# Scaling v on another engine, turning one pair later, and column tiles for the products of a lightning-attention kernel

## Chip, cores and metric

One core of one Trainium2 chip. The metric is device microseconds (us) of one execution; "span" is the time from the first to the last instruction in the trace, some 2 us less than the run's time. Runs of this program on one core scatter by up to 3%: the kernel before took 107.02 to 110.07 us in its first runs. Each comparison therefore uses runs of both kernels on the same chip, and runs more than 1.5% above the fastest of their kernel are left out as slow.

## The reference

Attention with decay, for 4 batches of 8 heads of 768 rows of 64, then a mixing layer over the tokens of each batch. Cut to what matters:

```python
# attention, per head, in blocks; lam is the head's decay
intra = ((qb @ kb.T) * Dmask) @ vb             # Dmask[i, j] = lam ** (i - j) for i >= j, else 0
inter = (qb * lam_pow) @ kv_state
out[block] = intra + inter
kv_state = lam_block * kv_state + (kb * rev_pow).T @ vb
# mixing, per batch: x is (768 tokens, 512 channels)
W_tok = (x @ w_q) @ (x @ w_k).T / 8
y = relu(W_tok @ x) @ w_out                    # f32, 4 x 768 x 512
```

Both kernels turn the decays into factors on q and v, so that a block needs only a mask of zeros and ones, and both reorder the mixing as `(x w_q) ((x w_k).T x)`.

## The kernel before

Two heads make a pair; there are 16 pairs `n`, four (`kk`) to each batch `b`. For each pair the kernel transposes q and k on TensorE (`turn`: trq, trk), scales v by powers of the decay (`scale_v`: vn), adds up the states (`states`: dps, then gs), multiplies q by k (`scores`: sc, masked to pr on VectorE), and adds `inter` and `values` into oa. `flip` transposes the result (xp to xnat). The mixing of a batch (`mix_...`) is laid among the pairs of the next ones: pq, pk, py, pm, and po, whose tile of 128 tokens is copied to osb and written out. Engines work in program order.

```python
    def scale_v(n, eng):
        ...
        eng.tensor_tensor(out=vn, in0=fv, in1=DvI[...].to_broadcast([128, 2, NCH, D]), op=ALU.mult)

    def mix_po(b, t, last=False):
        po = pst([128, HD], F32, "po")
        for kt in range(4):
            nc.tensor.matmul(po, M[b]["rmT"][:, kt, t * CH : (t + 1) * CH], wo[:, kt, :],
                             start=(kt == 0), stop=(kt == 3))
        osb = outp.tile([128, HD], F32, tag="osb", name="osb")
        ... # copied from po on ScalarE, or VectorE
        nc.sync.dma_start(out=out[b, t * CH : (t + 1) * CH, :], in_=osb)

    for n in range(N):
        b, kk = pairs[n]
        if n + 2 < N:
            take_k(n + 2)
            scale_v(n + 2, nc.gpsimd)          # two pairs ahead, on GpSimd
        if n + AHEAD < N:
            load(n + AHEAD)                    # AHEAD = 5, loads issued by GpSimd
        ...
        scores(n)
        ...
        if n >= 1:
            flip(n - 1)
        ...                                    # pq, py or po of earlier batches
        inter(n)
        values(n)
        if n + 1 < N:
            states(n + 1)
        if n + 2 < N:
            turn(n + 2)                        # two pairs ahead
        ...                                    # pk or pm
    ...                                        # tail: the last batch's mixing, six tiles of po
```

Of the kernel before, what the change touches and what calls it, by code (L numbers as in the profile page):

```python
# [21 lines left out]
AHEAD = 5  # L22
WARM = 11
# [3 lines left out]
def kernel(  # L27
# [14 lines left out]
    stage = ctx.enter_context(tc.tile_pool(name="stage", bufs=9))  # L42
# [7 lines left out]
    ps = ctx.enter_context(tc.tile_pool(name="ps", bufs=8, space=bass.MemoryType.PSUM))  # L50
# [19 lines left out]
    def load_q(n):  # L70
        t = stage.tile([128, 2, 3, 2 * D], BF16, tag="fq", name="fq")
        nc.gpsimd.dma_start(out=t, in_=q_rows(n))  # L72
        staged[n, "q"] = t

    def load_kv(n):
        for nm, src in (("k", k), ("v", v)):
            t = stage.tile([128, 2, NCH, D], BF16, tag="f" + nm, name="f" + nm)
            nc.gpsimd.dma_start(out=t, in_=kv_rows(n, src))  # L78
            staged[n, nm] = t

    def load(n):
        load_q(n)
        load_kv(n)


    load_q(0)
    t0 = stage.tile([128, 2, NCH, D], BF16, tag="fv", name="fv")
    nc.gpsimd.dma_start(out=t0, in_=kv_rows(0, v))
    staged[0, "v"] = t0
    lam_all = consts.tile([128, H], F32, name="lam_all")  # L90
    nc.sync.dma_start(out=lam_all, in_=lam.partition_broadcast(128))
    k0 = consts.tile([128, 2, NCH, D], F32, name="k0")
    nc.sync.dma_start(out=k0, in_=kv_rows(0, k))
    wqk_f = consts.tile([128, 2, 4, DHY], F32, name="wqk_f")
    for i, w in enumerate((moe_w_q, moe_w_k)):
        nc.sync.dma_start(out=wqk_f[:, i], in_=w.rearrange("(kt p) j -> p kt j", p=128))


    nc.scalar.preload_act_table_set("natural_log_exp_and_others")
    blank = consts.tile([128, HD], BF16, name="blank")  # L100
# [40 lines left out]
    load(2)  # L141
    lnl = consts.tile([128, H], F32, name="lnl")
    nc.scalar.activation(out=lnl, in_=lam_all, func=ACT.Ln)
    lnv = lnl.rearrange("p (k l) -> p k l", l=2)
    lncol = consts.tile([128, NP], F32, name="lncol")
    for hl in range(2):
        nc.vector.tensor_copy(
            out=lncol[hl * 64 : hl * 64 + 64, :], in_=lnv[hl * 64 : hl * 64 + 64, :, hl]
        )
# [6 lines left out]
    )  # L156
    Dq = [consts.tile([128, S], BF16, name=f"dq{kk}") for kk in range(NP)]
# [6 lines left out]
    swap = consts.tile([128, 128], BF16, name="swap")  # L164


    wqk = consts.tile([128, 4, 3 * DHY], BF16, name="wqk")
    wo = consts.tile([128, 4, HD], BF16, name="wo")

    def cast_wqk():  # L170
        nc.scalar.copy(out=wqk[:, :, 0:DHY], in_=wqk_f[:, 0])
        nc.scalar.copy(out=wqk[:, :, DHY : 2 * DHY], in_=wqk_f[:, 1])
        nc.scalar.copy(out=wqk[:, :, 2 * DHY :], in_=wqk_f[:, 0])
        nc.vector.tensor_copy(out=swap[:, 0:64], in_=ident[:, 64:128])
        nc.vector.tensor_copy(out=swap[:, 64:128], in_=ident[:, 0:64])

    def load_wo():
        nc.gpsimd.dma_start(out=wo, in_=moe_w_out.rearrange("(kt p) j -> p kt j", p=128))


    L = {}
    xT, xnat = {}, {}

    def take_k(n):
        if n == 0:
            kn = nat.tile([128, 2, NCH, D], BF16, tag="kn", name="kn")
            nc.vector.tensor_copy(out=kn, in_=k0)
        else:
            kn = staged.pop((n, "k"))
        L[n] = dict(kn=kn)  # L190

    def scale_v(n, eng):
        b, kk = pairs[n]
        vn = nat.tile([128, 2, NCH, D], BF16, tag="vn", name="vn")
        fv = staged.pop((n, "v"))
        eng.tensor_tensor(  # L196
            out=vn,
            in0=fv,
            in1=DvI[:, 2 * kk : 2 * kk + 2, :].unsqueeze(3).to_broadcast([128, 2, NCH, D]),
            op=ALU.mult,  # L200
        )
        L[n]["vn"] = vn

    def turn(n):
        b, kk = pairs[n]
        fq, kn = staged.pop((n, "q")), L[n]["kn"]
# [82 lines left out]
    def inter(n):  # L289
        gs = L[n]["gs"]  # L290
        oa = [pst([128, 3, CH], F32, "oa") for a in range(2)]
# [14 lines left out]
    def values(n):  # L306
# [5 lines left out]
        for a in range(2):  # L312
            for cc in range(3):
                c = 3 * a + cc
                for hl in range(2):
# [9 lines left out]
            nc.scalar.copy(  # L325
                out=xT[b][:, kk, a * HALF : (a + 1) * HALF].rearrange(
                    "d (c p r) -> d c r p", c=3, r=2
                ),
                in_=oa[a].rearrange("d c (r p) -> d c r p", r=2),
            )  # L330
        del L[n]

    def flip(n):
        b, kk = pairs[n]
        xp = pst([128, NCH, CH], BF16, "xp")
        for t in range(NCH):
            nc.tensor.transpose(xp[:, t, :], xT[b][:, kk, t * CH : (t + 1) * CH], ident)  # L337
        to = xnat[b][:, :, kk * CH : (kk + 1) * CH]
        if b == 0:
            nc.scalar.copy(out=to, in_=xp)  # L340
        else:
            nc.vector.tensor_copy(out=to, in_=xp)  # L342
# [6 lines left out]
    def mix_pq(b):  # L349
        qkT = hyp.tile([128, S], BF16, tag="qkT", name="qkT")  # L350
        M[b] = dict(qkT=qkT)
        for n in range(2):
            pq = pst([128, HALF], F32, "pq")
            for kt in range(NP):
                nc.tensor.matmul(  # L355
                    pq,
                    wqk[:, kt, n * DHY : n * DHY + 128],
                    xT[b][:, kt, n * HALF : (n + 1) * HALF],
                    start=(kt == 0),
                    stop=(kt == NP - 1),  # L360
                )
            nc.scalar.copy(out=qkT[:, n * HALF : (n + 1) * HALF], in_=pq)

    def mix_pk(b):
        qkT = M[b]["qkT"]
        pk = pst([128, NCH, CH], BF16, "pk")
        for t in range(NCH):
            nc.tensor.transpose(  # L368
                pk[:, t, :], qkT[:, t * CH : (t + 1) * CH], swap if t < 3 else ident
            )  # L370
        wkn = hyp.tile([128, NCH, 2, DHY], BF16, tag="wkn", name="wkn")
        nc.vector.tensor_copy(
            out=wkn, in_=pk[:, :, 0:DHY].unsqueeze(2).to_broadcast([128, NCH, 2, DHY])
        )
        M[b]["wkn"] = wkn

    def mix_py(b, last=False):
        py = pst([128, HD], F32, "py")
        for t in range(NCH):
            nc.tensor.matmul(  # L380
                py,
                M[b]["wkn"][:, t, :, :].rearrange("p i j -> p (i j)"),
                xnat[b][:, t, :],
                start=(t == 0),
                stop=(t == NCH - 1),
            )
        Y = hyp.tile([128, HD], BF16, tag="Y", name="Y")
        if last:
            nc.vector.tensor_copy(out=Y[:, 0:256], in_=py[:, 0:256])  # L389
            nc.scalar.copy(out=Y[:, 256:], in_=py[:, 256:])  # L390
        else:
            nc.scalar.copy(out=Y, in_=py)
# [3 lines left out]
    def mix_pm(b, dds, last=False):  # L396
        pms = {}
        for dd in dds:
            for n in range(2):
                r = slice(n * 64, n * 64 + 64)  # L400
                pm = pst([128, HALF], F32, "pm")
                nc.tensor.matmul(  # L402
                    pm,
                    M[b]["Y"][r, dd * CH : (dd + 1) * CH],
                    M[b]["qkT"][r, n * HALF : (n + 1) * HALF],
                    start=True,
                    stop=True,
                )
                pms[dd, n] = pm
        for n in range(2):  # L410
            for dd in dds:
                to = M[b]["rmT"][:, dd, n * HALF : (n + 1) * HALF]
                if last and dd % 2:
                    nc.vector.tensor_scalar(  # L414
                        out=to,
                        in0=pms[dd, n],
                        scalar1=1.0 / 8.0,
                        scalar2=0.0,
                        op0=ALU.mult,
                        op1=ALU.max,  # L420
                    )
                else:
                    nc.scalar.activation(  # L423
                        out=to, in_=pms[dd, n], func=ACT.Relu, scale=1.0 / 8.0
                    )

    def mix_po(b, t, last=False):
        po = pst([128, HD], F32, "po")
        for kt in range(4):
            nc.tensor.matmul(  # L430
                po,
                M[b]["rmT"][:, kt, t * CH : (t + 1) * CH],
                wo[:, kt, :],
                start=(kt == 0),
                stop=(kt == 3),
            )
        osb = outp.tile([128, HD], F32, tag="osb", name="osb")
        if last and t % 2:
# [3 lines left out]
        nc.sync.dma_start(out=out[b, t * CH : (t + 1) * CH, :], in_=osb)  # L442


    warm = pst([128, HD], F32, "warm")
    for _ in range(WARM):
        nc.tensor.matmul(warm, blank[:, 0:128], blank, start=True, stop=True)
    make_dq(0)
    take_k(0)
    turn(0)  # L450
    scale_v(0, nc.vector)
    states(0)
    make_dq(1)
    take_k(1)
    turn(1)
    load(3)
    scale_v(1, nc.vector)
    make_dq(2)
    load(4)

    for n in range(N):
# [6 lines left out]
        if n == 0:  # L468
            load_wo()
# [72 lines left out]
```

## Time and profile before

108.53 us (median of 3 runs); the profiled run took 107.25 us, with a span of 105.3 us.

| busy, us (share of span) | before |
|---|---|
| TensorE | 90.8 (86%) |
| VectorE | 66.4 (63%) |
| ScalarE | 67.9 (64%) |
| GpSimd | 68.6 (65%) |

The shares are averages over stages with different limits, so the prediction below reads the kernel by stages: a stage is cut where TensorE starts the scores of a batch's first pair.

The transfers themselves, in the view of that tile (line, engine, operation, count: shortest/median/longest issue in ns, first and last start):

```profile
L442 SPq DMA_DIRECT2D out_dram<-osb x24: 332/332/933, 45.6 to 102.1; - x24
```

SyncE issues 24 transfers of 128 rows, in 0.33 us each (one took 0.93), and the last six tiles come 0.91 us apart (5.49 us for the six in the chain). It has time to spare.

### The profile page before, as it was taken

What the parts mean: (1) busy time and instruction counts of PE and PEld (TensorE: products, weight loads), DVE (VectorE), ACT (ScalarE), POOL (GpSimd) and SP (SyncE); (2) the same over time, 40 slices, a digit from 0 to 9 for tenths busy, and PEclk for the clock granted to TensorE, in tenths of its full rate; (3) what the DMA queues carried; (4) which work ended last, traced back from release to release, by engine and by line L of the source; (5) the groups of instructions that cost most, each with busy time, mean ns of one, the idle gap of its engine ahead of it and who ended that gap; (6) DMA issues with size and microseconds to landing.
All of it is one profiled execution on the core that took longest, in us unless ns stands there. A gap on an engine that the chain in (4) does not pass through costs nothing. (4 is left out here: it accounts for less than half of the span.)

```text
span 105.3 us, 3311 instructions
## 1 busy us (share of the span) xinstructions
PE 90.8 (86%) x1403; PEld 58.5 (56%) x1403; DVE 66.4 (63%) x163; ACT 67.9 (64%) x123; POOL 68.6 (65%) x70
## 2 busy tenths in 40 slices
PE   5914878889699999999999999999999999989950
PEld 2213657658567577558757575577575555623410
DVE  2434587997594988918897829198986370237440
ACT  4045097987587397867839788778397868638320
POOL 5999999999999999999999999450410000000000
PEclk9995579999999999999999999999999999999999
DMA  0999999999999999999999999997000706332482
GB/s 15 195 167 165 165 160 166 165 163 166 200 167 167 162 165 162 163 178 219 231 169 162 160 175 233 237 200 242 4 0 6 290 9 253 146 121 84 166 321 111
DMA packets 67406, 16.93 MB, mean 161 GB/s; under 512 B 63808, under 2 KB 64320, under 8 KB 67392
## 3 DMA queue, kind: packets, MB, share of 16 engines
q0 software_dynamic: 61184, 9.77, 124.8%
q1 hardware_dynamic: 6208, 6.95, 19.9%
q8 instruction: 11, 0.18, 0.6%
q14 instruction: 3, 0.02, 0.1%
HBM read 20.19 MB, written 6.29 MB: 251 GB/s over the span
## 5 line engine op out<-in xcount | busy, mean ns | idle before, releaser
L285 DVE TENSOR_TENSOR pr<-sc,maskc 128x384 bf16<-128x384 f32 x64 | 31.1, 549 | 0.8 <-PE sc L273 0.3
L196 POOL TENSOR_TENSOR vn<-fv,DvI 128x768 bf16<-128x768 bf16 x14 | 21.0, 1500 | 7.0 <-DMA fv<-in_v_dram 4.6
L430 PE MATMUL po<-wo,rmT 128*128 128x512 bf16 x96 | 22.3, 379 | 0.0
L325 ACT CAST xT<-oa 128x384 bf16<-128x384 f32 x32 | 17.1, 594 | 2.9 <-PE oa L317 1.7
L230 ACT COPY kT<-trk 128x768 bf16<-128x768 bf16 x16 | 12.8, 798 | 8.5 <-PE trk L226 7.9
L441 ACT COPY osb<-po 128x512 f32<-128x512 f32 x21 | 12.3, 585 | 8.8 <-PE po L430 7.2
L78 POOL DMA_DIRECT2D fk<-in_k_dram x15 | 15.8, 1055 | 0.0
L78 POOL DMA_DIRECT2D fv<-in_v_dram x15 | 15.6, 1041 | 0.0
L72 POOL DMA_DIRECT2D fq<-in_q_dram x16 | 14.2, 889 | 0.8 <-POOLq L526 0.8
L253 DVE COPY two<-dps 128x64 f32<-128x64 f32 x16 | 3.6, 225 | 17.5 <-PE dps L243 17.4
L430 PEld LDWEIGHTS <-rmT 128*128 128x128 bf16 x96 | 9.1, 98 | 9.9 <-DVE rmT L414 0.5
L317 PE MATMUL oa<-pr,vn 128*64 128x128 bf16 x192 | 11.0, 223 | 2.4 <-DVE pr L285 1.7
L423 ACT ACTIVATE rmT<-pm 128x384 bf16<-128x384 f32 x28 | 11.6, 508 | 0.0
L273 PE MATMUL sc<-qT,kT 64*128 64x128 bf16 x192 | 10.3, 223 | 0.9 <-ACT kT L230 0.3
L211 PE MATMUL trq<-ident,fq 128*64 128x128 bf16 x192 | 9.0, 231 | 2.4 <-DMA fq<-in_q_dram 2.4
L217 DVE TENSOR_TENSOR qT<-trq,dq 128x768 bf16<-128x768 bf16 x16 | 8.8, 549 | 2.3 <-PE trq L211 2.2
L317 PEld LDWEIGHTS <-vn 128*64 128x64 bf16 x192 | 6.8, 109 | 5.6 <-issue 4.1
L342 DVE COPY xnat<-xp 128x768 bf16<-128x768 bf16 x12 | 6.6, 549 | 4.9 <-PE xp L337 4.9
L273 PEld LDWEIGHTS <-kT 64*128 64x128 bf16 x192 | 6.8, 96 | 4.0 <-issue 1.9
L337 PE MATMUL xp<-ident,xT 128*128 128x128 bf16 x96 | 8.1, 220 | 0.3
L211 PEld LDWEIGHTS <-fq 128*64 128x64 bf16 x192 | 6.6, 118 | 2.9 <-DMA fq<-in_q_dram 2.9
L226 PE MATMUL trk<-ident,fk 128*64 128x128 bf16 x180 | 8.0, 226 | 0.1
(57 smaller groups left out, 113.5 us busy)
## 6 DMA issues: line engine op xcount, KB each, us to landing
out_dram<-osb SPq DMA_DIRECT2D x24, 256.0 KB, 2.1
fq<-in_q_dram POOLq DMA_DIRECT2D x16, 192.0 KB, 6.8
fv<-in_v_dram POOLq DMA_DIRECT2D x16, 192.0 KB, 8.0
fk<-in_k_dram POOLq DMA_DIRECT2D x15, 192.0 KB, 7.8
wo<-in_moe_w_out_dram POOLq DMA_DIRECT2D x1, 512.0 KB, 9.2
k<-in_k_dram SPq DMA_DIRECT2D x1, 384.0 KB, 4.0
wqk_f<-in_moe_w_q_dram SPq DMA_DIRECT2D x1, 128.0 KB, 6.0
wqk_f<-in_moe_w_k_dram SPq DMA_DIRECT2D x1, 128.0 KB, 7.1
```

What stands on the lines that cost most here:

```text
L72: nc.gpsimd.dma_start(out=t, in_=q_rows(n))
L78: nc.gpsimd.dma_start(out=t, in_=kv_rows(n, src))
L196: eng.tensor_tensor(out=vn, in0=fv, in1=DvI[:, 2 * kk : 2 * kk + 2, :].unsqueeze(3).to_broadcast([128, 2, NCH, D]), op=ALU.mult,)
L211: nc.tensor.transpose(trq[hl * 64 : hl * 64 + 64, a, r, :], fq[:, hl, a, r * D : (r + 1) * D], ident,)
L230: nc.scalar.copy(out=kT, in_=trk)
L273: nc.tensor.matmul(sc[a, hl][:, cc, :], kT[r, c * CH : (c + 1) * CH], qchunk(n, r, c), start=True, stop=True, skip_group_check=True,)
L285: nc.vector.tensor_tensor(out=t, in0=sc[a, hl], in1=maskc, op=ALU.mult)
L317: nc.tensor.matmul(oa[a][r, cc, :], vn[:, hl, c, :], pr[a, hl][:, cc, :], start=False, stop=(cc == 2), skip_group_check=True,)
L325: nc.scalar.copy(out=xT[b][:, kk, a * HALF : (a + 1) * HALF].rearrange("d (c p r) -> d c r p", c=3, r=2), in_=oa[a].rearrange("d c (r p) - ...
L423: nc.scalar.activation(out=to, in_=pms[dd, n], func=ACT.Relu, scale=1.0 / 8.0)
L430: nc.tensor.matmul(po, M[b]["rmT"][:, kt, t * CH : (t + 1) * CH], wo[:, kt, :], start=(kt == 0), stop=(kt == 3),)
L441: nc.scalar.copy(out=osb, in_=po)
```

## The change

Its intent: VectorE takes the scaling of v, and GpSimd only issues loads; q and k are turned one pair ahead instead of two; the flip, the mixing's q and y products and its output products run as pairs of column tiles of TensorE, 64 output rows each; the mixing's k product comes out row-major, so that its transposes go; and what is left of the mixing is spread anew over the pairs.

```diff
-    ps = ctx.enter_context(tc.tile_pool(name="ps", bufs=8, space=bass.MemoryType.PSUM))
+    ps = ctx.enter_context(tc.tile_pool(name="ps", bufs=6, space=bass.MemoryType.PSUM))
+    psx = ctx.enter_context(tc.tile_pool(name="psx", bufs=2, space=bass.MemoryType.PSUM))   # oa
 # --- prologue: k0 through GpSimd, q0 and v0 in f32 through SyncE; cut ---
 # --- scale_v: eng.tensor_tensor -> nc.vector.tensor_tensor; values, two evictions: ---
-            nc.scalar.copy(
-                out=xT[b][:, kk, a * HALF : (a + 1) * HALF].rearrange(
-                    "d (c p r) -> d c r p", c=3, r=2
-                ),
-                in_=oa[a].rearrange("d c (r p) -> d c r p", r=2),
-            )
+            nc.scalar.copy(out=xT[b][:, kk, a * HALF : (a + 1) * HALF], in_=oa[a])
 # --- flip ---
-            nc.tensor.transpose(xp[:, t, :], xT[b][:, kk, t * CH : (t + 1) * CH], ident)
-        to = xnat[b][:, :, kk * CH : (kk + 1) * CH]
-        if b == 0:
-            nc.scalar.copy(out=to, in_=xp)
-        else:
-            nc.vector.tensor_copy(out=to, in_=xp)
+            for i in range(2):
+                o = t * CH + i * 64
+                nc.tensor.transpose(
+                    xp[i * 64 : i * 64 + 64, t, :], xT[b][:, kk, o : o + 64], ident
+                )
+        nc.scalar.copy(out=xnat[b][:, :, kk * CH : (kk + 1) * CH], in_=xp)
 # --- mix_pq, mix_pk -> mix_wk (row-major), mix_wq; mix_py, mix_pm on halves; cut ---
 # --- mix_po: four full products -> eight on column tiles; then the output: ---
-        nc.sync.dma_start(out=out[b, t * CH : (t + 1) * CH, :], in_=osb)
+        rows = out[b, t * CH : (t + 1) * CH, :].rearrange("(p r) d -> r p d", r=2)
+        for r in range(2):
+            nc.sync.dma_start(out=rows[r], in_=osb[r * 64 : r * 64 + 64, :])
 # --- the loop, with the placing of the mixing cut ---
-        if n + 2 < N:
-            take_k(n + 2)
-            scale_v(n + 2, nc.gpsimd)
-        if n + AHEAD < N:
-            load(n + AHEAD)
+        if n + 8 < N:
+            load(n + 8)
         scores(n)
-        if n >= 1:
-            flip(n - 1)
         inter(n)
+        if n + 1 < N:
+            take(n + 1)
+            turn(n + 1)
+            scale_v(n + 1)
+        if n >= 1:
+            flip(n - 1)
         values(n)
         if n + 1 < N:
             states(n + 1)
-        if n + 2 < N:
-            turn(n + 2)
```

The columns of the scores are in the order even rows, then odd rows. The kernel before put them back in order when it evicted oa. The changed one does not, and puts the rows in order with two output transfers for each tile of 128 tokens.

## The prediction

> **What bounds the kernel now.** I first read the page's slices, to see where the span has different limits.
>
> ```profile
> PE   5914878889699999999999999999999999989950
> DVE  2434587997594988918897829198986370237440
> ACT  4045097987587397867839788778397868638320
> POOL 5999999999999999999999999450410000000000
> PEclk9995579999999999999999999999999999999999
> ```
>
> Each digit is 2.6 us. TensorE is full from slice 11 (29 us) to slice 36; before that it has gaps while VectorE is fullest; GpSimd is full to 66 us. Then the timeline of TensorE, which I cut at the first scores of each batch of four pairs: 13.05, 29.18, 48.40 and 69.22 us, end of the last value products at 88.4. The stages are thus 13.05 (prologue), 16.1, 19.2, 20.8, 19.2 and 16.9 us (tail). A pair of the first batch looks like this (start, length, group):
>
> ```profile
> 21.20 0.51 PE L273 MATMUL sc<-qT,kT 64*128 64x128 bf16 x12
> 21.64 0.51 PE L337 MATMUL xp<-ident,xT 128*128 128x128 bf16 x6
> 22.08 0.47 PE L296 MATMUL oa<-qT,gs 64*64 64x128 bf16 x10
> 22.48 0.97 PE L317 MATMUL oa<-pr,vn 128*64 128x128 bf16 x7
> 23.70 0.33 PE L317 MATMUL oa<-pr,vn 128*64 128x128 bf16 x5 [0.25 <-DVE pr L285]
> 23.84 0.44 PE L243 MATMUL dps<-vn,fk 128*64 128x128 bf16 x10
> 24.09 0.53 PE L211 MATMUL trq<-ident,fq 128*64 128x128 bf16 x12
> 24.43 0.52 PE L226 MATMUL trk<-ident,fk 128*64 128x128 bf16 x12
> 24.89 0.51 PE L273 MATMUL sc<-qT,kT 64*128 64x128 bf16 x12
> ```
>
> Scores to scores is 3.69 us. TensorE waits for the four maskings (pr), then must run states and turning before the next scores: a loop through VectorE. Later the wait is gone; an extract of the third batch:
>
> ```profile
> 57.29 0.81 PE L273 MATMUL sc<-qT,kT 64*128 64x128 bf16 x12
> 58.17 0.49 PE L337 MATMUL xp<-ident,xT 128*128 128x128 bf16 x6
> 58.55 2.75 PE L430 MATMUL po<-wo,rmT 128*128 128x512 bf16 x12
> 61.23 0.47 PE L296 MATMUL oa<-qT,gs 64*64 64x128 bf16 x10
> ```
>
> Twelve output products take 2.68 us start to start. Here the sum of TensorE's work is the time. The groups by shape give the durations that I need below:
>
> ```profile
> L285 DVE TENSOR_TENSOR pr<-sc,maskc 128x384 bf16<-128x384 f32 x64 | 31.1, 549 | 0.8 <-PE sc L273 0.3
> L196 DVE TENSOR_TENSOR vn<-fv,DvI 128x768 bf16<-128x768 bf16 x2 | 1.9, 958 | 1.4 <-DMA fv<-in_v_dram 1.4
> L196 POOL TENSOR_TENSOR vn<-fv,DvI 128x768 bf16<-128x768 bf16 x14 | 21.0, 1500 | 7.0 <-DMA fv<-in_v_dram 4.6 <-PE trk L226 2.3
> L342 DVE COPY xnat<-xp 128x768 bf16<-128x768 bf16 x12 | 6.6, 549 | 4.9 <-PE xp L337 4.9
> ```
>
> The two VectorE scalings of v in the prologue already show what each of the sixteen will cost there: 958 ns. Back to back, an engine starts the next instruction sooner than a duration says: four maskings take 1.94 us, so 0.464 each; scaling v is followed 0.87 us later.
>
> **What the Trainium skill says.** "TensorEngine Tiling (Array Packing)", section Key Properties: changing the tiling mode drains TensorE. The trace agrees. Twelve products of 128 columns on column tiles (trq to trk) need 0.34 us, 28 ns each; twelve scores followed by the full-array transpose need 0.44; six transposes followed by pq, same mode, 0.35, and followed by inter, another mode, 0.44. A switch costs 0.1 us. The same page, section Restrictions, says that column tiling switches off the fast weight load; the trace has 98 ns for a weight load of the full array and 109 to 118 for 64 columns, which is small beside 512 streamed columns. "VectorE: DVE Perf Modes", section What auto-detection actually checks: two results a cycle only when every tensor is 16-bit. DvI is f32, so v runs at one element a cycle; 958 ns for 768 elements against 549 for the all-bf16 qT agrees. "DMA: Bandwidth & Descriptors", section SWDGE vs HWDGE vs iDMA: GpSimd computes the descriptors of its loads in software. Its rows show 0.89 to 1.06 us per issue, 3.0 a pair, with 1.5 for v in between.
>
> **The change part by part.**
>
> TensorE. (1) The flip becomes column tiles and stands beside turning and values, so a pair has 3 switches instead of 4, and the pair's own products fall from 2.67 us (0.25 states, 0.34+0.44 turn, 0.44 scores, 0.44 flip, 0.40 inter, 0.36 values) to about 2.55. (2) Per batch, pq computed both q and k twice over, 1.39; wq on column pairs is half, 0.65. The k product now comes out row-major (24 products of 64 columns, I take 28 to 57 ns each: 0.7 to 1.4) and saves the pk transposes (0.44). py duplicated its rows, 1.38; on column pairs 0.65. pm 0.66 stays about 0.65: one half in the scores' mode, one in inter's. po stays at 0.86 a tile, because two column tiles together stream what one full-array product did (trq at 28 ns against xp at 57 show that pairs really run together). Sum of a batch with six po tiles: before 20.8 as measured; after 4x2.55 + 1.1 + 0.65 + 0.65 + 0.65 + 5.2 + 0.2 of switches = 18.6. TensorE is given 2.2 us a batch.
>
> VectorE. v adds 0.87 to every pair, the flip's copy (0.46) goes to ScalarE. ScalarE per batch: kT 4x0.69, flip 4x0.69, xT 8x0.46, rmT 8x0.38, osb 6x0.48, wqT and Y 1.2, together about 16.5: not the bound.
>
> The new loop. In program order, after scores(n): VectorE masks four times, turns q(n+1), scales v(n+1); TensorE then needs that v for states(n+1); VectorE then copies the states (0.14+0.20+0.26) before it can mask n+1. From the scores' start: 0.37 to the first masking, 1.86 for four, 0.47 qT, 0.96 v, 0.06 to TensorE, 0.46 from states to their copy, 0.60 for the copies: the next masking starts at 4.78, so the period is 4.78 - 0.37 = **4.41 us** per pair. The old one was 3.69. TensorE's turn and flip now lie under the masking, and have room: 1.43 us for further products ahead of the states, and 0.34 between states and the next scores. What exceeds these two rooms lengthens the loop.
>
> Overhang by pair. kk=0: wk and wq fit, wkn costs VectorE 0.46, py exceeds by 0.3: 5.2. kk=1 and 2: six PSUM buffers for everything but oa make the second pm and the turning wait for maskings, 0.2; with two po tiles kk=1 is 5.45, and kk=2 with two po after the states (1.72 - 0.34) is 6.0; without them 4.6 each. kk=3: four po 6.1 (second batch), two 4.9, none 4.4. Batches: first 4x4.41 plus 0.5 for a cold clock = 18.1 (was 16.1); second 5.2+4.6+4.6+6.1 = 20.5 (was 19.2); third 5.2+5.45+6.0+4.9 = 21.6 (was 20.8); fourth 5.2+5.45+6.0 and a last pair of 2.75 = 19.4 (was 19.2). Together 79.6 against the 75.3 measured before: +4.3.
>
> Prologue. Scores(0) no longer stand behind turn(1), which took from 11.28 to 13.05. q0 comes through SyncE in f32 (k0 did: landing 4.0 us after issue), k0 through GpSimd (the first such load landed 6.2 us after issue, at 7.5). So trk at 7.8, states 8.5, four warming products, scores about 10.5: -2.5. It can hardly pay fully, because v(1) lands around 12 (13.4 before, behind one load more).
>
> Tail. One po tile more (0.86), pq and py halved (-1.4), last eviction split over two engines (-0.3), but eight pm in six PSUM buffers wait for their evictions where all eight fitted (+0.5): -0.3.
>
> Sum: 105.3 - 2.5 + 4.3 - 0.3 = 106.8 us of span, +1.4%.
>
> **The rivals.** (a) VectorE becomes the bound, as just worked out: +1%. For it speaks that the loop is serial; against it, that the author's uneven placing of po looks fitted to idle time. (b) TensorE stays the bound and the saved 2.2 us a batch show: three batches give -6 us, the prologue -2, about 99 us of time. That needs VectorE to overlap pairs, which its program order does not allow with v behind the maskings. Part of it may come. (c) The loads bound: in slices 2 to 10 the DMA moves 165 GB/s, 3.5 us a pair. At 4.4 us a pair this stays hidden after the first two pairs; it could only eat the prologue's gain. (d) TensorE idles 40% of the first batch and its clock falls, as it did in slices 3 to 5: +2 us, about 111.
>
> **Range and chances.** The runs before lie between 107.02 and 110.07, the profiled one at 107.25. +1.4 on that is 108.7, on the median 109.9. I choose a little below, 108.3, because (b) in part is likelier than (d). The range takes in a third of (b) and all of (d). Faster 0.28, same 0.48, slower 0.24.
>
> **What the new profile would show.** Right: first-batch scores 4.4 us apart with states waiting for VectorE's v; VectorE's waits for states the largest; TensorE's slices at 6 to 8 up to 30 us; GpSimd idle early. Wrong: scores 3.7 us or less apart in the first batch, or TensorE without gaps from 28 us on with a batch of 18 to 19 us; then (b) holds and my loop is mis-built. The weakest numbers are the cost of wk and the start of scores(0).

## More of the kernel before

One view that the prediction does not use belongs here, because it became decisive. It is the chain of waits that ended last, from 94 us on (start, length, what), of the kernel before:

```profile
95.00 0.90 PE pm L402 x8
...
95.91 5.49 PE po L430 x24
...
101.42 0.69 DVE osb L439
```

The tail is TensorE's, up to the last product; then one eviction and one transfer.

## The result

The changed kernel took 114.44 us (median of 4 runs, 114.31 to 114.61), beside 108.88 us for the kernel before (4 runs, two of them slow and left out of the ratio). The ratio is 1.062, with a 95% interval of 1.049 to 1.075: slower. A ratio in this text is the mean time of one kernel's fast runs over that of the other's in the same rounds, so it is not quite the ratio of the medians. The prediction of 108.3 us, with a range that was to take in its rival (d), "about 111", was wrong.

The slices of the changed kernel; each digit is 2.8 us here:

```profile
PE   5939965957878888989789979898997989999300
...
POOL 5999998699787468878327000000000000000000
```

Where TensorE had a row of nines before, from slice 11 on, it now has sevens and eights among them; GpSimd is done by slice 22, and the last two and a half slices (7 us) have no TensorE in them. VectorE in a pair of the first batch:

```profile
20.62 1.94 DVE L280 TENSOR_TENSOR pr<-sc,maskc 128x384 bf16<-128x384 f32 x4
22.48 0.55 DVE L212 TENSOR_TENSOR qT<-trq,dq 128x768 bf16<-128x768 bf16 x1
22.94 0.95 DVE L191 TENSOR_TENSOR vn<-fv,DvI 128x768 bf16<-128x768 bf16 x1
24.43 0.22 DVE L248 COPY two<-dps 128x64 f32<-128x64 f32 x1 [0.54 <-PE dps L238]
...
25.04 1.94 DVE L280 TENSOR_TENSOR pr<-sc,maskc 128x384 bf16<-128x384 f32 x4
```

TensorE over the same stretch, states and scores only:

```profile
23.94 0.45 PE L238 MATMUL dps<-vn,fk 128*64 128x128 bf16 x10 [1.00 <-DVE vn L191]
24.32 0.51 PE L268 MATMUL sc<-qT,kT 64*128 64x128 bf16 x12
...
28.36 0.45 PE L238 MATMUL dps<-vn,fk 128*64 128x128 bf16 x10 [1.00 <-DVE vn L191]
28.74 0.51 PE L268 MATMUL sc<-qT,kT 64*128 64x128 bf16 x12
```

The period is 25.04 - 20.62 = 4.42 us: masking, turning, scaling, then waiting for TensorE's states, in a ring. TensorE waits a full us for v in each turn.

The chain that ended last, in its final part:

```profile
101.59 0.60 SPq L451
...
102.29 0.54 SPq L451
...
102.87 2.45 DMA out_dram<-osb
...
105.44 0.44 DVE osb L443
```

And the transfers of the output tile, all of them (line, engine, operation, count: shortest/median/longest issue in ns, first and last start) and then the last eleven in SyncE's own timeline (start, length):

```profile
L451 SPq DMA_DIRECT2D out_dram<-osb x48: 466/591/778, 47.4 to 108.0; - x48
...
101.59 7.00 SPq L451 DMA_DIRECT2D out_dram<-osb  x11
```

Where TensorE alone stood in the chain before, there are now SyncE's issues, a transfer, and an eviction that waits for its buffer. The issues have doubled in number, and one of half as many rows takes longer, 0.59 us instead of 0.33. Eleven issues without a break take 7.00 us, so the two transfers of a tile need 2 x 0.64 = 1.27 us of SyncE, pauses between issues included, while TensorE delivers a tile every 0.90 us.

The two spans by stage (us). The tail is split where TensorE's last product ends.

| stage | before | predicted | after | after - before |
|---|---|---|---|---|
| to the first scores | 13.05 | 10.5 | 11.18 | -1.9 |
| batch 0 | 16.13 | 18.1 | 17.56 | +1.4 |
| batch 1 | 19.22 | 20.5 | 21.46 | +2.2 |
| batch 2 | 20.82 | 21.6 | 22.01 | +1.2 |
| batch 3 | 19.23 | 19.4 | 19.31 | +0.1 |
| tail, to the last product | 12.93 | | 13.19 | +0.3 |
| after the last product | 3.92 | | 7.39 | +3.5 |
| both parts of the tail | 16.85 | 16.6 | 20.58 | +3.7 |
| span | 105.3 | 106.8 | 112.1 | +6.8 |

So half of the loss is in the last 7 us, for which the prediction had one term, a last eviction split over two engines. The other half lies in the four batches, less what the prologue gave. Of the 3.5 us, 2.6 are the lateness of the last issue (3.30 us after the last product instead of 0.75), and 0.9 come after it (4.10 us from that issue to the end of the span instead of 3.16).

### The profile page after: what moved, and what is told of

Its sections match the earlier page's. It is cut to its first block, busy times and chain, and to the rows that moved or that the text cites. A ratio compares the mean times of both kernels' runs of the same rounds, so it can differ in the third digit from the quotient of the medians.

```text
span 112.1 us, 3971 instructions
## 1 busy us (share of the span) xinstructions
PE 88.8 (79%) x1706; PEld 59.0 (53%) x1706; DVE 71.1 (63%) x164; ACT 71.5 (64%) x136; POOL 48.1 (43%) x57
## 4 chain that ended last, share of the span: by engine, by line
PE 39%; DVE 33%; DMA 8%; ACT 7%; issue 4%; SPq 2%; DVEq 0%; ACTq 0%
DVE pr L280 16%; PE po L433 13%; DVE vn L191 9%; PE dps L238 5%; DMA v<-in_v_dram 5%; DVE qT L212 4%; PE trq L206 3%; PE py L376 2%; PE sc L268 2%; PE pm L406 2%; DMA out_dram<-osb 2%; ACT Y L391 2%; PE oa L291 2%; PE oa L312 2%; PE trk L221 2%
## 5 line engine op out<-in xcount | busy, mean ns | idle before, releaser
L225 ACT COPY kT<-trk 128x768 bf16<-128x768 bf16 x16 | 12.8, 798 | 19.5 <-PE trk L221 19.5
L433 PE MATMUL po<-wo,rmT 128*64 128x512 bf16 x192 | 23.2, 380 | 0.0
L448 ACT COPY osb<-po 128x512 f32<-128x512 f32 x21 | 12.4, 590 | 7.6 <-PE po L433 4.2
L320 ACT CAST xT<-oa 128x384 bf16<-128x384 f32 x32 | 14.4, 505 | 0.2 <-PE oa L312 0.2
L433 PEld LDWEIGHTS <-rmT 128*64 128x64 bf16 x192 | 10.3, 110 | 7.4 <-issue 0.5
L191 DVE TENSOR_TENSOR vn<-fv,DvI 128x768 bf16<-128x768 bf16 x15 | 14.2, 946 | 0.0
L332 ACT COPY xnat<-xp 128x768 bf16<-128x768 bf16 x16 | 12.9, 804 | 1.3 <-PE xp L329 1.3
L238 PE MATMUL dps<-vn,fk 128*64 128x128 bf16 (+2 forms) x160 | 7.3, 220 | 7.9 <-DVE vn L191 7.9
L426 ACT ACTIVATE rmT<-pm 128x384 bf16<-128x384 f32 x28 | 12.4, 492 | 0.6
L238 PEld LDWEIGHTS <-fk 128*64 128x64 bf16 x160 | 5.5, 111 | 9.8 <-DVE vn L191 8.8
L406 PE MATMUL pm<-wqT,Y 64*64 64x384 bf16 (+1 forms) x44 | 8.0, 328 | 2.1 <-ACT Y L391 1.3
L291 PE MATMUL oa<-qT,gs 64*64 64x128 bf16 x160 | 8.3, 227 | 0.4
L268 PE MATMUL sc<-qT,kT 64*128 64x128 bf16 x192 | 8.5, 223 | 0.0
```

The costliest lines, as they stand in the source:

```text
L191: nc.vector.tensor_tensor(out=vn, in0=L[n]["fv"], in1=DvI[:, 2 * kk : 2 * kk + 2, :].unsqueeze(3).to_broadcast([128, 2, NCH, D]), op=ALU.mult,
L225: nc.scalar.copy(out=kT, in_=trk)
L238: nc.tensor.matmul(dps[hl * 64 : hl * 64 + 64, c:end, :], kn[:, hl, c, :], vn[:, hl, c, :].unsqueeze(1).to_broadcast([128, end - c, D]), s ...
L320: nc.scalar.copy(out=xT[b][:, kk, a * HALF : (a + 1) * HALF], in_=oa[a])
L332: nc.scalar.copy(out=xnat[b][:, :, kk * CH : (kk + 1) * CH], in_=xp)
L426: nc.scalar.activation(out=to, in_=pms[n], func=ACT.Relu, scale=1.0 / 8.0)
```

## The experiments

Two theories. **The tail's theory:** the number of output issues on SyncE makes the 3.5 us at the end. Its rivals are the stride of the two transfers (every second row of the output) and the four output buffers. **The loop's theory:** v's scaling on VectorE makes the 4.9 us of the four batches. Its rival is that TensorE's own work in the new order makes it. Twelve kernels ran, on three chips, in three groups that share their runs of the kernel before; all gave correct results. "After" in the stage figures is the trace shown above; the experiments ran at other times and partly on other chips, so stage differences of a few tenths are not read as effects unless several runs repeat them.

### The output in one transfer

The reordering goes back to the eviction of oa, in the changed kernel; all else stays.

```diff
-            nc.scalar.copy(out=xT[b][:, kk, a * HALF : (a + 1) * HALF], in_=oa[a])
+            nc.scalar.copy(out=xT[b][:, kk, ...].rearrange("d (c p r) -> d c r p", c=3, r=2),
+                           in_=oa[a].rearrange("d c (r p) -> d c r p", r=2))
...
-        for r in range(2):
-            nc.sync.dma_start(out=rows[r], in_=osb[r * 64 : r * 64 + 64, :])
+        nc.sync.dma_start(out=out[b, t * CH : (t + 1) * CH, :], in_=osb)
```

> The changed kernel with the tokens back in natural order (the strided eviction of the kernel before) and one output DMA of 128 rows per tile in place of two of 64. Theory A (issue cost): SyncE needs 0.59 us for each of the last twelve issues, 7.1 us, more than the 5.4 us in which TensorE makes the last six tiles; with six issues of 0.33 us the stretch after the last matmul falls from 7.4 to about 3.9 us and the time by about 3.5 us (114.4 to 110.9). Rival B (the transfers of the end, or the four output buffers, are the limit whatever the number of issues): the stretch stays at 7 us and the time within 0.7 us. Everything before the last matmul: unchanged to within 0.5 us by both.

Measured: 110.80 us, before 107.70; ratio 1.030 (1.026 to 1.033). The output tile of this kernel:

```profile
L454 SPq DMA_DIRECT2D out_dram<-osb x24: 332/332/367, 47.5 to 105.6; - x24
```

After the last product there remain 4.15 us instead of 7.39, and the batches are the same to 0.1 us (17.45, 21.47, 22.12, 19.35). The two transfers cost 3.2 us of span, all at the end. The kernel is still 3% slower than the one before.

### The same two transfers in the kernel before

```diff
 # in the kernel before: oa evicted without reordering, and
-        nc.sync.dma_start(out=out[b, t * CH : (t + 1) * CH, :], in_=osb)
+        rows = out[b, t * CH : (t + 1) * CH, :].rearrange("(p r) d -> r p d", r=2)
+        for r in range(2):
+            nc.sync.dma_start(out=rows[r], in_=osb[r * 64 : r * 64 + 64, :])
```

> The kernel before with only the output part of the change: contiguous eviction of x and two output DMAs of 64 rows at a two-row stride per tile. Theory A: its tail grows as that of the changed kernel did, +3 to +3.5 us (ratio 1.03); the rest the same, since ScalarE, which gains 0.05 us an eviction, is no bound there. Rival B (the longer end of the changed kernel comes from its own schedule): within 0.7 us of the kernel before.

Measured: 110.33 us, before 107.32; ratio 1.030 (1.025 to 1.035). The end grew from 3.92 to 6.81 us, +2.9, and the median issue is 594 ns. (Batch 0 of this trace was 0.9 us longer too; its granted clock stayed at 0.50 until 19.9 us instead of 14.3.) The cost belongs to the transfers, in either kernel, and not to the new order of work.

### Two transfers without the stride

The eviction of oa reorders again, and each transfer takes 64 neighbouring rows.

```diff
-            nc.sync.dma_start(out=rows[r], in_=osb[r * 64 : r * 64 + 64, :])
+            o = t * CH + r * 64
+            nc.sync.dma_start(out=out[b, o : o + 64, :], in_=osb[r * 64 : r * 64 + 64, :])
```

> The changed kernel with the tokens in natural order, but still two output DMAs of 64 rows per tile, each now to 64 consecutive rows of the output. Theory A1 (the number of issues costs, whatever the layout): each issue still takes 0.5 to 0.6 us of SyncE, the stretch after the last matmul stays at 6.5 to 7.4 us, time about 114. Theory A2 (the two-row stride of the destination makes an issue dear): an issue falls to the 0.33 us of the kernel before or less, the stretch to 4 to 4.5, time about 111.

Measured: 115.06 us, before 107.32; ratio 1.074 (1.068 to 1.079). The end is 7.37 us. The output tile of this kernel:

```profile
L456 SPq DMA_DIRECT2D out_dram<-osb x48: 466/594/622, 48.3 to 109.1; - x48
```

The stride is not the cause; the number of transfers is.

### Eight output buffers

```diff
-    outp = ctx.enter_context(tc.tile_pool(name="outp", bufs=4))
+    outp = ctx.enter_context(tc.tile_pool(name="outp", bufs=8))
```

> The changed kernel with eight output buffers instead of four, nothing else. Theory A (SyncE's issue rate is the limit of the tail): the last evictions no longer wait for a buffer, but the issues stand just as dense: time within 0.7 us of 114.4. Rival B (the landing of an output with only four buffers is the limit): the stretch after the last matmul falls from 7.4 to about 4.5 us, time about 111.5.

Measured: 113.87 us, before 107.32; ratio 1.065 (1.057 to 1.073). The last tile's first half is now evicted at 104.9 us instead of 105.4, yet the last issue starts at 108.1 and the end is 7.37 us. So the wait for a buffer that the chain of the changed kernel shows is a consequence: with it gone, SyncE is as late as before. The last twelve issues start from 101.20 to 108.11 us, 0.63 us apart, one behind the other. A last rival is that the transfers themselves set the pace. In the trace of the changed kernel each of the last twelve that has a landing on record landed 2.25 to 2.45 us after the start of its issue, the last like the first; transfers that pile up would land later and later. What an issue does during its 0.59 us the trace does not show.

### Half of the output through GpSimd

```diff
-            nc.sync.dma_start(out=rows[r], in_=osb[r * 64 : r * 64 + 64, :])
+            (nc.sync, nc.gpsimd)[r].dma_start(out=rows[r], in_=osb[r * 64 : r * 64 + 64, :])
```

> The changed kernel with the second of the two output DMAs of each tile issued by GpSimd, which is idle in the tail; same transfers, same number. Theory A (issue cost on SyncE): SyncE has six issues of 0.59 us for the last six tiles, less than TensorE needs; the stretch after the last matmul falls from 7.4 to 4 to 4.5 us, the time by about 3 us. Rival B (the transfers are the limit): no change, within 0.7 us.

Measured: 121.99 us, before 107.70; ratio 1.134 (1.131 to 1.137). A miss for every theory. The waits of this kernel (us in total, times, longest):

```profile
POOL out_dram L451 <- ACT osb L448: 39.3, 17, 9.0
...
ACT osb L448 <- DMA out_dram<-osb: 9.2, 2, 7.9
...
PE sc L268 <- ACT osb L448: 7.1, 1, 7.1
```

GpSimd works in program order too. Where it stands before an output whose tile is not ready, its loads stand behind it, and an output stands behind loads; a buffer came free late, ScalarE waited for it, and TensorE then stood still for 7.1 us in batch 2. In the tail the end took 6.37 us, 1.0 less than in the changed kernel, but evictions waited for transfers there as well. It is not a clean test of the tail, and I do not use it as one.

### v on GpSimd, two pairs ahead

In the changed kernel; to keep GpSimd's order as it was, the loads go back to five pairs ahead as well (so do the loads ahead of the loop; that part of the edit is cut).

```diff
-        if n + 8 < N:
-            load(n + 8)
+        if n + 2 < N:
+            take(n + 2)
+            scale_v(n + 2, nc.gpsimd)
+        if n + 5 < N:
+            load(n + 5)
...
             turn(n + 1)
-            scale_v(n + 1)
+            if n == 0:
+                scale_v(1)
```

> The changed kernel with only the scaling of v (pairs 2 to 15) back on GpSimd, two pairs ahead, and the loads paced five ahead as before. Theory A (the loop through VectorE with v in it sets the time of batches): without the 0.87 us of v states no longer wait for VectorE, and batches 2 to 4 become what TensorE's work is: about 18.3, 19.5 and 17.5 us in place of 21.5, 22.0 and 19.2; the first batch stays near 17, now paced by GpSimd (4.5 us a pair). Time falls by 6 to 8 us. Rival B (ScalarE with the flip's copy, or column-tiled products, set the batches): the time falls by less than 2 us. The tail of 7.4 us stays in both.

Measured: 109.91 us, before 107.70; ratio 1.020 (1.014 to 1.026). That is about 4.5 us under the changed kernel's 114.44 (4.0 by the spans of the two traces), in the direction of the loop's theory but short of the size it gave. The batches took 17.62, 20.32, 19.96 and 18.60 us (17.56, 21.46, 22.01, 19.31): batches 1 to 3 gain 3.9 us, batch 0 none. Two reasons can be read. In batch 0, GpSimd paces: states wait up to 1.65 us for its v. Later, ScalarE does, once the VectorE loop is open; from the fourth pair of batch 1, on TensorE:

```profile
42.03 0.51 PE L269 MATMUL sc<-qT,kT 64*128 64x128 bf16 x12
43.11 0.74 PE L292 MATMUL oa<-qT,gs 64*64 64x128 bf16 x10 [0.57 <-ACT xT L321]
```

So VectorE was the bound, and behind it, close, stood ScalarE, to which the change had given the flip's copy.

### v on VectorE, but ahead of the maskings

`scale_v(n + 1)` moves from behind `turn(n + 1)` to ahead of `scores(n)`, for n from 2 on. VectorE does the same work, in an order in which TensorE's states do not wait for it.

```diff
+        if 2 <= n < N - 1:
+            take(n + 1)
+            scale_v(n + 1)
         scores(n)
...
-            take(n + 1)
-            turn(n + 1)
-            scale_v(n + 1)
+            if n < 2:
+                take(n + 1)
+            turn(n + 1)
+            if n < 2:
+                scale_v(n + 1)
```

> The changed kernel with one change of order: from pair 2 on, v of the next pair is scaled ahead of the maskings of this pair instead of behind them. Same work on every engine. Theory A (the order puts v between masking and states, and VectorE idles while TensorE does the products behind the states): v moves into that idle time; the first batch gains only the 0.14 us a pair that VectorE waits for states, later pairs up to 0.87; together 4 to 6.5 us less. Rival B (VectorE's amount of work, not its place in the order, is what costs): less than 2 us.

Measured: 113.69 us, before 107.70; ratio 1.057 (1.052 to 1.063): less than 1 us below the changed kernel, where I had expected 4 to 6.5, so a miss. The last two pairs of batch 0, the first with the new order, take 4.1 us instead of 4.4, and batches 2 and 3 gain 1.0 and 0.8 us, but batch 1 loses 2.05 us. On TensorE there:

```profile
34.58 0.30 PE L376 MATMUL py<-xnat,wkn 128*64 128x256 bf16 x2 [1.50 <-issue]
```

TensorE stood still for 1.50 us waiting for nothing that the trace shows, and its granted clock was 0.50 from 36 to 38 us. So the order alone gains a little where nothing else happens; how much, this run does not settle.

### v on VectorE in the kernel before

```diff
-            scale_v(n + 2, nc.gpsimd)
+            scale_v(n + 2, nc.vector)
```

> The kernel before with only the scaling of v moved to VectorE, two pairs ahead and in front of the maskings, where it stands in program order there. Theory A (v costs where VectorE sets the loop, and only there): in the first batch a pair takes 3.69 + 0.87 = 4.5 us, +2 to +3.3 us in all, nothing in the later batches, where VectorE idles for up to 2.5 us a pair and TensorE is full: ratio 1.02 to 1.03. Rival B (v on VectorE costs in every pair): +8 us or more.

Measured: 117.08 us, before 107.31; ratio 1.092 (1.087 to 1.097): +9.8 us. That is the size that rival B gave, not the +2 to +3.3 us of theory A. But two things are mixed in it. On TensorE, in the first pair:

```profile
18.17 0.27 PE L317 MATMUL oa<-pr,vn 128*64 128x128 bf16 x1 [4.01 <-DVE pr L285]
```

v of pair 2 stands in front of the first maskings and waits for its load, and the maskings with it: that pair took 9.06 us instead of 4.46. Later pairs of batch 0 took 4.1 to 4.6 us (starts 21.73, 25.86, 30.40, 34.95) instead of 3.7 to 4.3, with the granted clock at 0.50 until 24.8 us instead of 14.3. And batches 1 to 3 lost 1.2 us each, where theory A expected nothing: the scaling costs TensorE time there too, although VectorE is not full in them (busy 17.4 of 20.4 us in batch 1). The run gives no clean size for batch 0.

### v on GpSimd and the output in one transfer

The edits of "The output in one transfer" and of "v on GpSimd" together.

> The run before last kernel of this study (v on GpSimd, one output DMA, flip's copy on VectorE: 104.64 us) with only the flip's copy left on ScalarE, as the change has it. Theory A (the copy on ScalarE makes the eviction of x late and TensorE waits for it in inter): 106 to 106.8 us, 1.5 to 2 us more, and TensorE waits of about 0.5 us for ScalarE's x in the fourth pair of a batch. Rival B (it lies beside other work): 104.3 to 105.

Measured: 107.47 us, before 107.31; ratio 1.003 (0.996 to 1.010). The two causes together bring the changed kernel back to the level of the one before. Stages: 10.99, then 18.44, 20.42, 20.26, 19.21, then 13.18 and 4.12; this trace is of the slowest of the four runs, 108.33 us.

### And the flip's copy back on VectorE

The same, and the copy of xp from batch 1 on goes back from ScalarE to VectorE:

```diff
-        nc.scalar.copy(out=xnat[b][:, :, kk * CH : (kk + 1) * CH], in_=xp)
+        to = xnat[b][:, :, kk * CH : (kk + 1) * CH]
+        if b == 0:
+            nc.scalar.copy(out=to, in_=xp)
+        else:
+            nc.vector.tensor_copy(out=to, in_=xp)
```

> The changed kernel's schedule and column-tiled products with three parts undone: v on GpSimd (from pair 2), one output DMA in natural order, and the flip's copy back on VectorE from the second batch on. Theory A (these three are the losses, the rest of the change is a gain): -3.5 for the output, -4.5 for v as measured each alone, and another -1 to -2 because ScalarE's queue no longer holds up the eviction of x on which the next inter waits: 104.5 to 105.5 us, ratio about 0.975. Rival B (flip on VectorE gives nothing, or the parts overlap): 106.5 or more, no better than 0.99.

Measured: 104.64 us, before 107.32; ratio 0.980 (0.969 to 0.990). This beats both kernels; whether by the full 2%, the interval leaves open. Stages: 11.34, then 17.29, 19.23, 19.62, 18.04, then 13.19 and 4.14. TensorE is busy 18.99 of the 19.62 us of batch 2: what the changed kernel took from TensorE's work shows, once neither VectorE nor ScalarE nor SyncE is in its way. Against the kernel without this edit it is 2.8 us (medians, of two chips; 2.3% by the two ratios). The two traces lie further apart, 3.8 us: 3.0 of it in batches 1 to 3, and 1.1 in batch 0, which the edit does not touch, less 0.35 before the first scores.

### The flip as full-array products

The last kernel, with the flip's twelve half transposes as six full ones again. Everything else stays on column tiles, so each pair gets two more changes of tiling mode.

```diff
-            for i in range(2):
-                o = t * CH + i * 64
-                nc.tensor.transpose(xp[i * 64 : i * 64 + 64, t, :], xT[b][:, kk, o : o + 64], ident)
+            nc.tensor.transpose(xp[:, t, :], xT[b][:, kk, t * CH : (t + 1) * CH], ident)
```

> The kernel with v on GpSimd, one output DMA and the flip's copy on VectorE (104.64 us), with the flip's transposes over the full array again, between the column-tiled turn and the column-tiled products. Theory A (a change of the tiling mode costs TensorE 0.1 us): two switches more per pair, 0.2 us, in some twelve pairs that TensorE bounds: +2 to +2.5 us. Rival B (switches are hidden, or the shorter weight loads of column tiles cost as much): within 0.7 us.

Measured: 106.62 us, before 107.31; ratio 0.994 (0.990 to 0.998), 2.0 us more than with half transposes (medians, of two chips; 1.4% by the two ratios). TensorE with halves (the kernel of the experiment before), in batch 2:

```profile
64.39 0.50 PE L222 MATMUL trk<-ident,fk 128*64 128x128 bf16 x12
64.72 0.50 PE L335 MATMUL xp<-ident,xT 128*64 128x128 bf16 x12
65.06 1.03 PE L443 MATMUL po<-wo,rmT 128*64 128x512 bf16 x8
```

And with the full array:

```profile
65.69 0.50 PE L222 MATMUL trk<-ident,fk 128*64 128x128 bf16 x12
66.13 0.51 PE L333 MATMUL xp<-ident,xT 128*128 128x128 bf16 x6
66.57 1.05 PE L439 MATMUL po<-wo,rmT 128*64 128x512 bf16 x8
```

trk to xp takes 0.33 us in one mode and 0.44 into another, and xp to po 0.34 and 0.44. In batches 1 to 3, where TensorE is the bound, two such changes in each of 12 pairs come to 12 x 2 x 0.1 = 2.4 us. Measured, these batches took 19.62, 20.53 and 18.72 us instead of 19.23, 19.62 and 18.04, together 2.0 us more.

### An attempt at the best version

The kernel with the flip's copy on VectorE, but v of pairs 1 to 4 scaled on VectorE and only the later ones on GpSimd, and the two copies of Y in the other order.

```diff
+            if n >= 3:
+                scale_v(n + 2, nc.gpsimd)
...
+        if n in (2, 3):
+            scale_v(n + 1)
         scores(n)
...
-        for i in range(2):
+        for i in (1, 0):
             o = slice(64 - i * 64, 128 - i * 64)
```

> An attempt at the best of both: as the 104.64 us kernel, but v of pairs 1 to 4 on VectorE, ahead of the maskings from pair 3 on, so that GpSimd's 4.5 us a pair no longer paces the first batch; and the half of Y that the first pm needs copied first. Theory: the first batch falls from 17.3 to about 16.5 us, and three times 0.27 us at pm: 103 to 103.7 us. If the first batch is bound by the arrival of the loads instead: no better than 104.3.

Measured: 106.92 us, before 107.31; ratio 0.992 (0.983 to 1.000). A miss. Batch 0 took 17.39 us and gained nothing, since xp waited 0.95 us for ScalarE's kT, and two standstills appeared, of which this is one:

```profile
34.13 0.30 PE L386 MATMUL py<-xnat,wkn 128*64 128x256 bf16 x1 [0.79 <-issue]
```

### A stall with no wait shown

Standstills of TensorE of over 0.25 us that are put down to "issue" occur in seven of the fourteen traces, twelve in all: in the changed kernel (0.33 and 0.77 us), in the one with v early (1.50 and 0.47), in the last one (0.79 and 0.96), and in the four that change only the output of the changed kernel. There are none in the kernel before or in the best version. The trace file shows what they have in common. Number TensorE's recorded instructions, weight loads included, by their start, from 0: all twelve stalls end with instruction 961, 1217, 1473, 1729 or 2497, which is 193 plus a multiple of 256. The packets of the trace's queue q8, "instruction", have 16384 bytes each, and there are 13 of them for 3421 such instructions in the changed kernel and 11 for 2812 in the one before. Take the packets and these places in order: in all fourteen traces an instruction at such a place starts 1.29 us or more after the end of its packet, the twelve stalls end 1.30 to 1.61 us after it, and in the kernel before the least is 1.67. So TensorE very probably waited for its own instructions, of which the changed kernel has more (1706 products with as many weight loads, where the one before had 1403). No run varied that by itself, so what it costs is not measured.

## Why the prediction was wrong

**The step that failed is the tail: "-0.3".** The prediction summed "One po tile more (0.86), pq and py halved (-1.4), last eviction split over two engines (-0.3)" and a wait for PSUM buffers (+0.5). The diff's loop of two transfers has no term in it. TensorE's part of the tail was nearly right (+0.3). But 48 issues of 0.59 us in place of 24 of 0.33 left SyncE behind a TensorE that delivers tiles faster than SyncE can issue them. The tail came out 3.7 us longer, where 0.3 less was predicted. That is 4.0 of the 5.3 us between the predicted span, 106.8, and the measured one. One transfer took 3.2 us of it back, two transfers added 2.9 us to the kernel before, and neither the stride nor the buffers changed it. The term "last eviction split over two engines (-0.3)" failed as well: the two halves ran one after the other (VectorE for 0.42 us, then ScalarE, which waited for it, for 0.37), so that with one transfer the last eviction ended 0.87 us after the last product, against 0.73 for the undivided one before. What could have been read beforehand: the tail's pace, 0.91 us a tile, beside the 0.33 us of an issue. It left room for two issues at the old duration, so only a doubt about the duration of an issue of half as many rows would have shown the risk. Its 0.59 us was in no view of the kernel before.

**The loop was right, and in size.** "4.41 us per pair" was measured as 4.42, with a wait for v in each. The overhangs held too. Predicted and measured pairs: batch 1, 5.2, 4.6, 4.6, 6.1 and 5.54, 4.55, 4.41, 6.96; batch 2, 5.2, 5.45, 6.0, 4.9 and 5.67, 5.57, 5.82, 4.95; batch 3, 5.2, 5.45, 6.0, 2.75 and 5.21, 5.58, 5.81, 2.71. Batches 1 and 2 contain the two stalls, 1.1 us together. The sum was +4.9 where +4.3 was predicted. In part the nearness is luck: the 4.3 holds 0.5 for a cold clock that did not come, and the 4.9 holds the stalls, which no term foresaw; without both, 3.8 stands against 3.8. The 5.45 of kk = 1 does not follow from the terms shown (4.41, 0.2 and one po beyond its room, 0.52, give 5.13). So rival (a), VectorE as the bound, is what happened; rival (d), a falling clock in batch 0, did not (granted clock 0.97 there, and 1.00 from 12.4 us on).

**TensorE's saving was less than "2.2 us a batch".** In the best version, where TensorE is the bound, batch 2 with its six po tiles took 19.62 us against 20.82 before: 1.2 us. The disputed term, the row-major k product, took 0.80 us (24 products, 33 ns each), within the 0.7 to 1.4 allowed. I had also called ScalarE "not the bound" by its sum of 16.5 us a batch; as a sum that stands (17.28 of 22.01 us in batch 2), but with v off VectorE its late copies were what TensorE waited for, and moving the flip's copy back was worth 2.8 us by the medians.

**The prologue gave 1.9 of "-2.5" us.** The first scores started at 11.18 us, not at 10.5. trk started at 8.04 (7.8 predicted) and the states at 8.83 (8.5); the four warming products, at a granted clock of 0.50 from 9.0 us on, then held TensorE from 9.35 to 11.18.

**The choice of the time.** The text placed its time a little below what its own sum gave, because part of rival (b) seemed likelier than (d); it also added 1.4 us, the figure of the per cent, where its sum was 1.5. No part of (b) came while v was in VectorE's loop. Even a sum that was right about the loop could not have reached 114.4 without the output's issues. Without them, the kernel took 110.8 us, below the "about 111" that the range was to take in.

## What to carry to other kernels

Count the issues of every queue in the last stage, as you count products: a transfer split in two moved no more bytes, but cost 3 us where tiles came faster than they could be issued. An instruction moved to an engine with idle time is free only if no other engine waits for it in the same ring: here 0.9 us of work on VectorE, which had idle time, placed between the maskings and the states, went with 4.42 us for a pair of batch 0 instead of 3.69, and taking it off gave 3.9 us in the twelve pairs of the later batches. When one bound is taken away, look at once at the next engine's waits, since here ScalarE stood right behind VectorE, and the saving on TensorE showed only after both, and SyncE, were out of the way.

## What the Trainium skill lacked or had wrong

- "DMA: Bandwidth & Descriptors", section Issuing engines are not separate DMA queues, calls the time to initiate a DMA "usually small relative to the DMA itself". Here it set the end of the kernel: 0.59 us for each transfer of 64 rows issued from SyncE back to back (0.47 where it was not), against 0.33 us for one of 128 rows. The page gives the issue of a copy only as one number of cycles for "previous generations", whatever the shape; I found none by shape for this chip. Why half the rows take longer to issue, and whether part of it is waiting for the transfers before, these runs leave open. The same page's section Rules for kernel authors says not to split a transfer into two partition halves; it is right, and the runs show a price for it, 2.9 to 3.2 us.
- "TensorEngine Tiling (Array Packing)", section Key Properties, says that changing the mode drains TensorE, without a figure: 0.1 us a change here, and 2.0 us more in batches 1 to 3 when each pair has two more.
- "TensorE: Matmul & The Clock Gate", section What's actually happening, has the clock fall after an idle window of about 3.4 us. Shorter standstills were followed by half clock here: after 1.50 us without work at 33 us in one kernel (TensorE busy 2.1 of the 4 us from 32 to 36; granted clock 0.50 from 35.8 to 39.2 us), and after 1.64 us at 22 us in the best version (0.50 from 24.9 to 28.3 us). But 1.65 us at 22 us in the kernel with only v on GpSimd were not (1.00 from 12.8 us on), so the length alone does not decide it. The changed kernel waited 1.00 us in each pair of batch 0 and kept 1.00 from 12.4 us on.
- "Runtime: NRT & Kernel Launch", section Instruction fetch mechanics, has instructions fetched in blocks of 16 KiB, 256 instructions each, and calls the cost of crossing into the next block "mostly hidden". Here all twelve standstills of TensorE of 0.26 to 1.50 us with no wait shown end at instructions that lie a multiple of 256 apart, and 1.30 to 1.61 us after a packet of 16384 bytes in the instruction queue.
